# Attention scores on TensorE: a shared 128-row product over padded keys becomes twelve 64-row products

## The chip, the cores and the metric

The kernel runs on one core of a Trainium2 chip. The metric is the device time in microseconds (us) of one execution, the median of several. TensorE is called PE, its weight loads PEld, VectorE DVE, ScalarE ACT, GpSimd POOL, and SyncE, which issues the transfers, SP.

## The reference

An attention layer with a learned relative-position bias feeds a two-layer network. With 4 batches, 8 heads, 576 positions and a head dimension of 64:

```
scores = q @ k.T / 8                                   # 4 x 8 x 576 x 576
x      = log1p(|i - j|) / log1p(max(i, 1))
scores = scores + relu(x * w1 + b1) @ w2               # a bias for each head
attn   = softmax(scores)
h      = (attn @ v), heads side by side                # 2304 x 512
out    = relu(h @ w_in)**2 @ w_out                     # 512 -> 2048 -> 512
```

## The kernel before

Two batches are worked on together, as a pair `p`; batch `b` of the pair has its 64 head dimensions on partitions 64b to 64b+63, for queries and for keys. The 576 query rows of a batch are cut into chunks `c`: chunks 1 to 4 have 128 rows of each batch (the full blocks), chunk 0 has the last 64 rows of both batches together. A step `n` is one (pair, chunk, head); there are 2 x 5 x 8 = 80, and 64 of them are of full blocks. The order of all work is written out by hand in a string, `PROGRAM`, whose words name a piece of work and its argument ("qk:12", "kz:0.3"); every engine keeps that order.

Queries and keys are split into two 16-bit halves, so that a score is a sum of three products (`terms`: high x high, high x low, low x high). `qk(n)` makes the scores of a step in the PSUM tile `sc`, three banks of 512 columns, of which there is one. `softmax_a(n)` (L661) lets DVE add the bias, find the row minimum of the negated scores and write both batches' 576 columns to SBUF, one instruction for each batch; ACT then takes the exponential (L674). Later come the transposition (`turn` on PE for the first 16 steps, a transposing transfer after that), `pv` (L762, attention times values), and for each chunk the network: `g1` (L842), `square` (L854, L856, L862) and `g2` (L875).

For a full block, `qk` puts the scores of batch 0 at columns 0 to 575 of `sc` and those of batch 1 at columns 960 to 1535. So 512 columns of batch 0 fill bank 0, 512 of batch 1 fill bank 2, and the 64 columns left of each lie in bank 1. The part in bank 1 is made first, for both batches at once (L638): three products over all 128 partitions with 128 columns, whose moving operand `kz` holds batch 0's last 64 keys in its first 64 partitions and columns, batch 1's first 64 keys in the others, and zeros elsewhere. The other part follows as six products over 64 partitions each (L643), with 512 columns, alternating between the batches; `tile_position` puts the two batches on the upper and the lower half of the PE array.

`kz` is zeroed once by DVE (L903). `k_pad`, the word "kz" in `PROGRAM`, copies the keys of one head into it with two ACT instructions (L321), after `k_split` has made the halves on POOL or DVE; there are 16 heads in all (8 for each pair).

Of the kernel before, what the change touches and what calls it, by code (L numbers as in the profile page):

```python
# [9 lines left out]
F16 = mybir.dt.float16  # L10
# [19 lines left out]
ENG = {'kh': 'PPPPPPPAPPPPPPPP', 'kl': 'PPPPPPPPDDDDDDDD', 'vh': 'PPPPPPPAPPPPPPPP', 'vl': 'PPPPPPPPDDDDDDDD', 'wh': 'AAAAAAAA', 'wl': 'PPPPPPPP', 'wc': 'OOOOOOOO', 'wp': '01010101', 'qh': 'PPPPPPDDDDDDPPPPPPPP', 'ql': 'DDDDDDDDDDDDDDDDDDDD', 'ev': 'AAAAAAAAAAAAAAAAAAAAAAAAAAAADDDDDDDD', 'er': 'AAAAAAAAAAAAAAAAAAAAAAAAAAAADDDDDDDD', 'gh': 'PPPPPPPPPPPPPPPPDDDDDDDDDDDDDDDDDDDDDDDDDDDDDDDDDDDDDDDDDDDDDDDDDDDDDDDDDDDDDDDD', 'gl': 'PPPPPPPPPPPPPPPPPPPPPPPPPPPPPPPPPPPPPPPPPPPPPPPPPPPPPPPPPPPPPPPPPPPPPPPPPPPPPPPP', 'al': 'PPPPPPPPPPPPPPPPPPPPPPPPPPPPPPPPPPPPPPPPPPPPPPPPPPPPPPPPPPPPPPPPPPPPPPPPPPPPPPPP', 'oe': 'AAAAAAAAAAAAAAAAAAAA', 'kz': 'AAAAAAAAAAAAAAAA', 'te': 'AAAAAAAAAAAAAAAAAAAAAAAAAAAAAAAAAAAAAAAAAAAAAAAAAAAAAAAAAAAAAAAAAAAAAAAAAAAAAAAA', 'tt': 'AAAAAAAAAAAAAAAAAAAAAAAAAAAAAAAAAAAAAAAAAAAAAAAAAAAAAAAAAAAAAAAAAAAAAAAAAAAAAAAA', 'xe': 'AAAAAAAAAAAAAAAAAAAA', 'ah': 'AAAAAAAAAAAAAAAAAAAAAAAAAAAAAAAAAAAAHAAHAAHAAHAAHAAHAAHAAHAAHAAHAAHAAHAAHAAHAAHAAAA'}  # L30
# [6 lines left out]
NKZ = 8  # L37
# [6 lines left out]
BONE = False  # L44
PROGRAM = (
# [155 lines left out]
def tile_attention_moe(  # L201
# [99 lines left out]
    def k_split(p, h):  # L301
# [8 lines left out]
        else:  # L310
            nc.vector.scalar_tensor_tensor(
                out=t[:, 1, :], in0=st, scalar=float(2 ** KS), in1=t[:, 0, :],
                op0=ALU.mult, op1=ALU.subtract)

    def k_pad(p, h):
        t = k_t[p, h]
        for b in range(2):
# [687 lines left out]
```

## Time and profile before

| | |
|---|---|
| median of three runs | 639.39 us (638.95 to 641.38) |
| the profiled execution, its own time | 638.85 us |
| its span, first to last instruction | 637.2 us |
| mean granted clock of PE | 0.985 |
| busy: PE, PEld, DVE, ACT, POOL | 94%, 61%, 67%, 59%, 60% of the span |

The span begins with the first instruction and ends with the last; 1.65 us of the execution's time lie around it. A matmul's end is modelled from its size, and its duration covers the way through the array, so that matmuls that follow each other overlap in the listing; the distance from one start to the next is the better measure of what a matmul costs.

### The profile page before, as it was taken

The numbers are of one execution on the slowest core, as the hardware profiler recorded it, in microseconds if no ns is written. First come the engines' busy times: TensorE is split into PE (matmuls) and PEld (weight loads), VectorE is DVE, ScalarE is ACT, GpSimd is POOL, SyncE is SP. The second block draws the span as 40 slices with busy tenths as digits, with TensorE's granted clock in tenths as the row PEclk, the third lists the DMA queues.
The fourth block names the chain that finished last, engine by engine and source line by source line (L and its number), as shares of the span: only waits on it lengthen the run. The fifth ranks groups of instructions, "written<-read, shape, count | busy, mean of one in ns | idle before, by whom it ended". The sixth has DMA issues, their size and how long they took to land.

```text
span 637.2 us, 15498 instructions
## 1 busy us (share of the span) xinstructions
PE 601.6 (94%) x6056; PEld 385.7 (61%) x6056; DVE 426.4 (67%) x840; ACT 376.3 (59%) x811; POOL 384.8 (60%) x389
## 2 busy tenths in 40 slices
PE   5578998899999999999999999999999999999997
PEld 2135575664666477557556765766676676577564
DVE  7999999998679795787874663566456363613321
ACT  5679997769676365755567455746636575214020
POOL 5785599999766345766965646555665556523211
PEclk9779999999999999999999999999999999999999
DMA  8999987888799877798879768559975889512000
GB/s 289 342 309 294 284 257 229 259 192 186 167 193 199 181 167 181 162 235 200 191 159 231 149 130 185 133 115 192 183 142 121 150 172 163 121 39 71 17 34 17
DMA packets 204264, 112.16 MB, mean 176 GB/s; under 512 B 166816, under 2 KB 179104, under 8 KB 204192
## 3 DMA queue, kind: packets, MB, share of 16 engines
q1 hardware_dynamic: 204192, 111.18, 73.7%
q8 instruction: 47, 0.77, 0.5%
q14 instruction: 25, 0.20, 0.1%
HBM read 55.44 MB, written 15.61 MB: 111 GB/s over the span
## 4 chain that ended last, share of the span: by engine, by line
PE 67%; POOL 12%; DVE 7%; DMA 6%; issue 4%; ACT 3%; SPq 1%; POOLq 0%; DVEq 0%; ACTq 0%
PE o L875 25%; PE hp L842 25%; PE pv L762 7%; PE sc L643 5%; DMA kst<-kd 3%; POOL v L278 2%; DVE s L661 2%; PE bp L554 2%; DVE hg L489 2%; POOL cv L278 2%; POOL v L345 2%; PE sc L633 1%; POOL winL L406 1%; POOL g L862 1%; PE sc L638 1%
## 5 line engine op out<-in xcount | busy, mean ns | idle before, releaser
L842 PE MATMUL hp<-xt,winH 128*128 128x256 f16 (+1 forms) x1280 | 193.2, 262 | 1.4 <-DVE r L856 1.3
L875 PE MATMUL o<-woutH,g 128*128 128x512 f16 x576 | 184.8, 380 | 1.7 <-POOL g L862 1.0
L842 PE MATMUL hp<-xt,winL 128*128 128x256 f16 (+1 forms) x640 | 161.7, 262 | 0.0
L862 POOL TENSOR_TENSOR g<-r,g 128x512 f16<-128x512 f32 (+1 forms) x80 | 88.8, 1113 | 91.4 <-DVE g L280 78.6
L875 PEld LDWEIGHTS <-g 128*128 128x128 f16 x864 | 79.5, 98 | 98.9 <-issue 9.4
L842 PEld LDWEIGHTS <-winH 128*128 128x128 f16 x1280 | 117.9, 98 | 25.3 <-issue 8.5
L717 POOL TENSOR_TENSOR a<-s,a 128x1024 f16<-128x1024 f32 (+1 forms) x64 | 132.5, 2070 | 0.0
L661 DVE CUSTOM_DVE_ANT_0 s<-sc,bt 128x576 f32<-128x576 f32 x144 | 104.6, 749 | 35.3 <-PE sc L643 13.7
L856 DVE TENSOR_TENSOR r<-hp,r 128x512 f32<-128x512 f32 (+1 forms) x80 | 50.7, 634 | 108.4 <-ACT r L854 107.9
L875 PE MATMUL o<-woutL,g 128*128 128x512 f16 x288 | 109.2, 379 | 0.0
L674 ACT ACTIVATE s<-s,nm 128x576 f32<-128x576 f32 x120 | 92.9, 775 | 6.4 <-ACT nm L672 0.4
L854 ACT ACTIVATE r<-hp 128x512 f32<-128x512 f32 (+1 forms) x80 | 43.7, 546 | 85.9 <-PE hp L842 83.1
L715 POOL TENSOR_TENSOR a<-s,a 128x128 f16<-128x128 f32 (+1 forms) x64 | 29.8, 465 | 105.7 <-ACT a L276 76.2
L762 PE MATMUL pv<-v,at 128*128 128x64 f16 (+5 forms) x2112 | 88.0, 203 | 2.4 <-ACT at L276 1.3
L672 ACT ACTIVATE nm<-mx,esc 128x1 f32<-128x1 f32 x120 | 34.4, 287 | 77.9 <-DVE mx L661 77.5
L276 ACT ACTIVATE a<-s 128x1152 f16<-128x1152 f32 (+1 forms) x64 | 70.3, 1099 | 13.2 <-DMA at<-a 12.2
L842 PEld LDWEIGHTS <-winL 128*128 128x128 f16 x640 | 62.6, 98 | 5.8
L762 PEld LDWEIGHTS <-at 128*128 128x128 f16 (+1 forms) x1792 | 55.0, 100 | 16.8 <-issue 10.6
L489 DVE TENSOR_SCALAR hg<-tab_t 128x464 f32<-128x464 f32 (+17 forms) x88 | 60.0, 712 | 0.1
L280 DVE TENSOR_SCALAR g<-r 128x512 f16<-128x512 f32 (+1 forms) x64 | 46.6, 730 | 17.1 <-PE o L875 16.1
L643 PE MATMUL sc<-k,q 64*128 64x512 f16 x384 | 52.6, 379 | 0.0
L554 PE MATMUL bp<-hg,w2s 128*32 128x288 f32 (+15 forms) x152 | 36.3, 532 | 8.6 <-ACT hg L481 3.3
(90 smaller groups left out, 707.3 us busy)
## 6 DMA issues: line engine op xcount, KB each, us to landing
bt<-biasd SPq DMA_DIRECT2D x64, 288.0 KB, 3.6
stg<-w_in SPq DMA_DIRECT2D x16, 512.0 KB, 4.7
stg<-w_out SPq DMA_DIRECT2D x16, 512.0 KB, 5.6
biasd<-be SPq DMA_DIRECT2D x16, 295.5 KB, 5.3
bt<-biasd SPq DMA_DIRECT2D x32, 144.0 KB, 4.3
qst<-qd SPq DMA_DIRECT2D x32, 128.0 KB, 3.6
out<-o SPq DMA_DIRECT2D x16, 256.0 KB, 2.8
v<-vd SPq DMA_DIRECT2D x8, 320.0 KB, 7.0
```

Of the source, the lines that this page charges most:

```text
L276: nc.scalar.activation(out=out, in_=in_, func=AF.Copy, scale=scale)
L489: nc.vector.tensor_scalar(ht, src, scl[:, n:n + 1], None, op0=ALU.min)
L554: nc.tensor.matmul(out=bp[32 * t:32 * t + 32, 0:n], lhsT=w2s if gi < 4 or t < z else w2n, rhs=hg[gi, t][:, a0:a1, :] if gi in ONEP else hg ...
L643: nc.tensor.matmul(out=sc[:, 1024 * b:1024 * b + 512], lhsT=qt[r, qz, qs], rhs=kt[r, z, 64 * b:64 * b + 512], start=(m == 0), stop=(m == 2 ...
L661: nc.vector.tensor_tensor_reduce(s[:, 576 * b:576 * b + 576], sc[:, 960 * sb:960 * sb + 576], bt, inv, 3.0e38, ALU.add, ALU.min, mx[:, b:b ...
L674: nc.scalar.activation(out=sl, in_=sl, func=AF.Exp, scale=-1.0, bias=mx[:, b:b + 1] if f32 else nm[:, b:b + 1], accum_out=su[:, h, b:b + 1])
L717: eng.tensor_tensor(av[:, :, 640:1152], ev[:, :, 0:512], av[:, :, 0:512], op=ALU.subtract)
L762: nc.tensor.matmul(out=dst, lhsT=lhsT, rhs=rhs, start=b not in [x[1] for x in seq[:j]], stop=b not in [x[1] for x in seq[j + 1:]], tile_po ...
L842: nc.tensor.matmul(out=hp[:, f * T:f * T + T].rearrange("p (b t) -> p b t", b=nb), lhsT=wt[:, k, c0:c0 + 128], rhs=xt[:, 0:nb, z * 4 + k, ...
L856: nc.vector.tensor_tensor(rr, hp[:, 0:2 * T], rr, op=ALU.mult)
L862: eng.tensor_tensor(g[:, 1, 0:2 * T], rr, g[:, 0, 0:2 * T], op=ALU.subtract)
L875: nc.tensor.matmul(out=blk["o", b], lhsT=g[:, z, c0:c0 + 128], rhs=wt[:, 2 * u + f, :], start=(u == 0 and f == 0 and z == 0 and wt is wout ...
```

## The change

The padded copies are gone: the tile `kz`, its zeroing, `k_pad`, and the 32 words "kz" in `PROGRAM`. The other words keep their order.

The scores of batch 0 now lie at columns 64 to 639 of `sc`, those of batch 1 at 896 to 1471. Each batch has 448 columns in a bank of its own and 128 in bank 1. They are made with twelve products over 64 partitions each, in the order `SEQ`; an entry is (batch, own bank or not, term). While batch 0 makes its three products of 128 columns in bank 1, batch 1 begins with 448 columns in bank 2; at the end batch 1 makes its 128 columns in bank 1 while batch 0 finishes in bank 0. Both halves of the array write to bank 1, at different times: a `drain` behind batch 0's third product increments the semaphore `bank`, and PE waits for it ahead of batch 1's first product there. `fusable=True` allows the compiler to delete that drain and to put its increment on the instruction ahead of it.

```diff
+TM = 128
+SO = [512 - S + TM, 1024 - TM]
+SEQ = [(0, 0, 0), (1, 1, 0), (0, 0, 1), (0, 0, 2), (0, 1, 0), (1, 1, 1), (0, 1, 1), (1, 1, 2), (0, 1, 2),
+       (1, 0, 0), (1, 0, 1), (1, 0, 2)]
...
-    kz = const.tile([128, NKZ, 2, 128], F16, name="kz")
...
-    def k_pad(p, h):
-        t = k_t[p, h]
-        for b in range(2):
-            r = slice(64 * b, 64 * b + 64)
-            src = t[r, :, 512 - 512 * b:576 - 512 * b]
-            if zn("kz", p * 8 + h) == "A":
-                nc.scalar.activation(out=kz[r, h % NKZ, :, r], in_=src, func=AF.Copy)
-            else:
-                nc.vector.tensor_copy(kz[r, h % NKZ, :, r], src)
-            if b == 0:
-                yield
...
+    bank_sem, bank_n = ctx.enter_context(nc.semaphore("bank")), [0]
+    nc.tensor.sem_clear(bank_sem)
...
-            mid = sc[:, 512:1408].rearrange("p (b j) -> p b j", b=2)[:, :, 0:64]
-            for m, (qz, z) in enumerate(terms):
-                nc.tensor.matmul(out=mid, lhsT=qt[:, qz, qs], rhs=kz[:, h % NKZ, z, :],
-                                 start=(m == 0), stop=(m == 2))
-            for m, (qz, z) in enumerate(terms):
-                for b in range(2):
-                    r = slice(64 * b, 64 * b + 64)
-                    nc.tensor.matmul(out=sc[:, 1024 * b:1024 * b + 512], lhsT=qt[r, qz, qs],
-                                     rhs=kt[r, z, 64 * b:64 * b + 512],
+            for b, own, m in SEQ:
+                if (b, own, m) == (1, 0, 0):
+                    bank_n[0] += 1
+                    nc.tensor.wait_ge(bank_sem, bank_n[0])
+                r = slice(64 * b, 64 * b + 64)
+                if b:
+                    k0, w = (TM, S - TM) if own else (0, TM)
+                else:
+                    k0, w = (0, S - TM) if own else (S - TM, TM)
+                o = SO[b] + k0
+                qz, z = terms[m]
+                i = nc.tensor.matmul(out=sc[:, o:o + w], lhsT=qt[r, qz, qs], rhs=kt[r, z, k0:k0 + w],
                                      start=(m == 0), stop=(m == 2), tile_position=(64 * b, 0))
+                if (b, own, m) == (0, 0, 2):
+                    nc.tensor.drain(fusable=True).then_inc(bank_sem, 1)
...
-            sb = b if c else h % 2
+            sb = SO[b] if c else 960 * (h % 2)
             nc.vector.tensor_tensor_reduce(
                 s[:, 576 * b:576 * b + 576],
-                sc[:, 960 * sb:960 * sb + 576], bt, inv, 3.0e38, ALU.add, ALU.min, mx[:, b:b + 1])
+                sc[:, sb:sb + 576], bt, inv, 3.0e38, ALU.add, ALU.min, mx[:, b:b + 1])
...
-        nc.vector.memset(kz, 0.0)
-        yield
```

## Rows read from the trace of the kernel before

**Rows 1.** The page: busy time, share of the span, instructions.
```profile
PE 601.6 (94%) x6056; PEld 385.7 (61%) x6056; DVE 426.4 (67%) x840; ACT 376.3 (59%) x811; POOL 384.8 (60%) x389
```

**Rows 2.** Busy time of each engine in stretches of the span.
```profile
core 0: us, PE busy (x) PEld busy (x) DVE busy (x) ACT busy (x) POOL busy (x), PEclk, DMA share, GB/s
...
90.00:120.00 30.00, 26.49 (x240) 17.41 (x238) 28.24 (x57) 24.02 (x53) 28.37 (x37) 1.00 0.81 240
...
320.00:380.00 60.00, 59.98 (x666) 41.17 (x664) 36.06 (x77) 36.06 (x76) 33.74 (x28) 1.00 0.82 170
```

**Rows 3.** Waits of PE, 155 to 530 us: total us, times, longest.
```profile
PE hp L842 <- DVE r L856: 1.3, 1, 1.3
PE pv L762 <- DMA at<-a: 1.0, 1, 1.0
PE o L875 <- POOL g L862: 0.3, 1, 0.3
```

**Rows 4.** The chain that ended last: by engine, then pieces (start, us).
```profile
PE 67%; POOL 12%; DVE 7%; DMA 6%; issue 4%; ACT 3%; SPq 1%; POOLq 0%; DVEq 0%; ACTq 0%
...
63.90 0.75 PE sc L643 x6
...
70.04 0.75 PE sc L643 x6
...
165.10 0.27 PE sc L638 x3
165.37 0.75 PE sc L643 x6
166.13 0.92 PE pv L762 x28
...
518.45 0.75 PE sc L643 x6
```

**Rows 5.** Line 643 on PE in stretches: length, busy (count), clock.
```profile
60.00:155.00 95.00, 10.68 (x78) 1.00 0.82 239
155.00:320.00 165.00, 17.25 (x126) 1.00 0.85 186
320.00:520.00 200.00, 24.64 (x180) 1.00 0.78 159
```

**Rows 6.** PE's timeline round one step, from narrow windows: start, us.
```profile
309.86 0.38 PE L875 MATMUL o<-woutH,g 128*128 128x512 f16 x1
310.08 0.22 PE L638 MATMUL sc<-kz,q 128*128 128x128 f16 x1
...
310.13 0.28 PE L638 MATMUL sc<-kz,q 128*128 128x128 f16 x2
...
310.19 0.22 PE L638 MATMUL sc<-kz,q 128*128 128x128 f16 x1
310.34 0.82 PE L643 MATMUL sc<-k,q 64*128 64x512 f16 x6
...
310.78 0.38 PE L643 MATMUL sc<-k,q 64*128 64x512 f16 x2
311.09 0.39 PE L842 MATMUL hp<-xt,winH 128*128 128x256 f16 x2
```

**Rows 7.** Groups: line, engine, shape, count; busy us, mean ns; idle before.
```profile
L643 PE MATMUL sc<-k,q 64*128 64x512 f16 x384 | 52.6, 379 | 0.0
...
L638 PE MATMUL sc<-kz,q 128*128 128x128 f16 x192 | 21.2, 219 | 1.4 <-DVE mx L661 1.4
...
L321 ACT ACTIVATE kz<-k 64x128 f16<-64x128 f16 x32 | 9.8, 305 | 8.1 <-POOL k L309 4.4 <-DVE k L311 3.3
...
L903 DVE MEMSET kz<- 128x1024 uint32 x1 | 0.9, 912 | 0.2 <-issue 0.2
```

**Rows 8.** The chain's pieces up to 80 us: start, us.
```profile
46.69 0.20 ACT kz L321
46.90 0.31 ACT kz L321
...
49.49 0.20 ACT kz L321
49.70 0.31 ACT kz L321
...
75.95 0.63 POOL cv L278
```

**Rows 9.** The drains at the kernel's end on PE's queue: ns min/median/max, starts.
```profile
L1001 PEldq DRAIN  x2: 13/1496/2978, 629.6 to 636.7; - x2
```

**Rows 10.** PE's timeline, its last matmuls.
```profile
631.95 0.38 PE L875 MATMUL o<-woutL,g 128*128 128x512 f16 x1
632.16 0.38 PE L875 MATMUL o<-woutH,g 128*128 128x512 f16 x1
```

More of the change, by code (lines that the diff above doesn't have):

```diff
@@ L27 @@
 LB = 1152
-ENG = {'kh': 'PPPPPPPAPPPPPPPP', 'kl': 'PPPPPPPPDDDDDDDD', 'vh': 'PPPPPPPAPPPPPPPP', 'vl': 'PPPPPPPPDDDDDDDD', 'wh': 'AAAAAAAA', 'wl': 'PPPPPPPP', 'wc': 'OOOOOOOO', 'wp': '01010101', 'qh': 'PPPPPPDDDDDDPPPPPPPP', 'ql': 'DDDDDDDDDDDDDDDDDDDD', 'ev': 'AAAAAAAAAAAAAAAAAAAAAAAAAAAADDDDDDDD', 'er': 'AAAAAAAAAAAAAAAAAAAAAAAAAAAADDDDDDDD', 'gh': 'PPPPPPPPPPPPPPPPDDDDDDDDDDDDDDDDDDDDDDDDDDDDDDDDDDDDDDDDDDDDDDDDDDDDDDDDDDDDDDDD', 'gl': 'PPPPPPPPPPPPPPPPPPPPPPPPPPPPPPPPPPPPPPPPPPPPPPPPPPPPPPPPPPPPPPPPPPPPPPPPPPPPPPPP', 'al': 'PPPPPPPPPPPPPPPPPPPPPPPPPPPPPPPPPPPPPPPPPPPPPPPPPPPPPPPPPPPPPPPPPPPPPPPPPPPPPPPP', 'oe': 'AAAAAAAAAAAAAAAAAAAA', 'kz': 'AAAAAAAAAAAAAAAA', 'te': 'AAAAAAAAAAAAAAAAAAAAAAAAAAAAAAAAAAAAAAAAAAAAAAAAAAAAAAAAAAAAAAAAAAAAAAAAAAAAAAAA', 'tt': 'AAAAAAAAAAAAAAAAAAAAAAAAAAAAAAAAAAAAAAAAAAAAAAAAAAAAAAAAAAAAAAAAAAAAAAAAAAAAAAAA', 'xe': 'AAAAAAAAAAAAAAAAAAAA', 'ah': 'AAAAAAAAAAAAAAAAAAAAAAAAAAAAAAAAAAAAHAAHAAHAAHAAHAAHAAHAAHAAHAAHAAHAAHAAHAAHAAHAAAA'}
+ENG = {'kh': 'PPPPPPPAPPPPPPPP', 'kl': 'PPPPPPPPDDDDDDDD', 'vh': 'PPPPPPPAPPPPPPPP', 'vl': 'PPPPPPPPDDDDDDDD', 'wh': 'AAAAAAAA', 'wl': 'PPPPPPPP', 'wc': 'OOOOOOOO', 'wp': '01010101', 'qh': 'PPPPPPDDDDDDPPPPPPPP', 'ql': 'DDDDDDDDDDDDDDDDDDDD', 'ev': 'AAAAAAAAAAAAAAAAAAAAAAAAAAAADDDDDDDD', 'er': 'AAAAAAAAAAAAAAAAAAAAAAAAAAAADDDDDDDD', 'gh': 'PPPPPPPPPPPPPPPPDDDDDDDDDDDDDDDDDDDDDDDDDDDDDDDDDDDDDDDDDDDDDDDDDDDDDDDDDDDDDDDD', 'gl': 'PPPPPPPPPPPPPPPPPPPPPPPPPPPPPPPPPPPPPPPPPPPPPPPPPPPPPPPPPPPPPPPPPPPPPPPPPPPPPPPP', 'al': 'PPPPPPPPPPPPPPPPPPPPPPPPPPPPPPPPPPPPPPPPPPPPPPPPPPPPPPPPPPPPPPPPPPPPPPPPPPPPPPPP', 'oe': 'AAAAAAAAAAAAAAAAAAAA', 'te': 'AAAAAAAAAAAAAAAAAAAAAAAAAAAAAAAAAAAAAAAAAAAAAAAAAAAAAAAAAAAAAAAAAAAAAAAAAAAAAAAA', 'tt': 'AAAAAAAAAAAAAAAAAAAAAAAAAAAAAAAAAAAAAAAAAAAAAAAAAAAAAAAAAAAAAAAAAAAAAAAAAAAAAAAA', 'xe': 'AAAAAAAAAAAAAAAAAAAA', 'ah': 'AAAAAAAAAAAAAAAAAAAAAAAAAAAAAAAAAAAAHAAHAAHAAHAAHAAHAAHAAHAAHAAHAAHAAHAAHAAHAAHAAAA'}
 PATS = ["DDDD", "ADDD", "AADD", "DDDP", "DDPP", "ADDP", "ADPP", "AADP", "AAPP", "DPPP"]
@@ L36 @@
 ORDER = [[0, 3, 2, 4, 1], [1, 4, 2, 3, 0]]
-NKZ = 8
 NF = 16
@@ L942, in tile_attention_moe @@
     work = {"st": start, "tb": tables, "sc": scales, "hc": hconst, "rs": rowscale, "hg": hgen, "bm": bias_mm,
-            "bo": bias_out, "bl": bias_ld, "qd": q_dma, "qs": q_split, "kd": k_dma, "ks": k_split, "kz": k_pad,
+            "bo": bias_out, "bl": bias_ld, "qd": q_dma, "qs": q_split, "kd": k_dma, "ks": k_split,
             "vd": v_dma, "vs": v_split, "wd": w_dma, "ws": w_split, "qk": qk, "sa": softmax_a, "sb": softmax_b,
```

295 rows, old and new, of the table PROGRAM are left out of this document.

## The prediction

> **What bounds the kernel now.** I read the page's busy times first, then the stretches, PE's waits, the chain, and last the start times of single matmuls inside one step. The page says that PE is busy for 94% of the span and that no other engine passes 67% [rows 1]. An average over stages is not yet a bound, so the stretches come next: from 90 to 120 us POOL and DVE each work 28 of 30 us while PE has more air; from 320 to 380 us PE is busy 59.98 of 60 us, while DVE and ACT work 36.06 each and POOL less [rows 2]. The boundary is near 155 us. From there to 530 us PE waits 2.6 us in all for other engines, in three places [rows 3]. So in the second stage a microsecond of PE work is nearly a microsecond of time, and in the first it is not.
>
> The chain says the same and counts for me. 67% of it is PE. Between 160 and 530 us it runs through the scores of 43 steps; the first piece, with the mid products before it, and the last are shown, and in the first stage two more steps are on it [rows 4]. Line 643 has six matmuls a step, so the 126 and 180 of the stretches are 51 steps in the second stage, and the 78 ahead of it are 13 [rows 5]. Eight of the 51 therefore lie beside a stretch in which something else came last.
>
> **What one step costs now.** The timeline gives it to two decimals [rows 6]. The three mid products start at 310.08, 310.13 and 310.19, so 128 columns cost 0.055 us. The first 64-row product starts 0.15 after the last mid product, 0.095 more than its columns need: going from 128 rows to 64 costs that much. The pairs start at 310.34 and the third pair at 310.78, so a pair, two products of 512 columns on the two halves, costs 0.22 (line 875's 512 columns cost 0.215, [rows 10]); the halves really run side by side. From the last pair to the next line's first matmul are 0.31, which is 0.095 over the pair's columns: the way back to 128 rows. The sum is 0.11 + 0.15 + 0.44 + 0.31 = 1.01; the chain's pieces give 0.27 + 0.75 = 1.02 [rows 4]. I take 1.02. The step into the mid products is free: 310.08 less 309.86 is just the 512 columns before.
>
> **What one step will cost.** All twelve products are 64-row ones. The price of going to 64 rows is still paid once, now at the front: 0.095. The columns scale: 448 cost 0.215 x 448/512 = 0.188, 128 cost 0.055. Batch 0's half has 3 x 0.055 + 3 x 0.188 = 0.73; batch 1's half has the same work in another order. If the two halves run freely beside each other the step's columns take 0.73 instead of 0.11 + 0.055 + 0.65, and the way back is 0.095 again. Sum: 0.095 + 0.73 + 0.095 = 0.92, so 0.10 less by these rounded figures, and I use 0.095. There are three more weight loads a step; in `pv` 28 load-and-multiply pairs take 0.92, so a pair can follow another in 0.033, below the 0.055 of the shortest product here [rows 4]. I cost the loads at nothing; if 64-row loads could not run ahead, three times 0.033 would eat the gain.
>
> **The semaphore.** If the compiler puts the increment on batch 0's third product, no instruction is left that holds PE. That product starts about 0.11 into the columns; as modelled it ends 0.22 later [rows 7], at 0.33. Batch 1's first product in bank 1 is due when its two further products of 448 columns are through, at 3 x 0.188 = 0.56. The wait is over 0.2 us ahead of its turn: nothing. Queued behind it on PE are only this step's last two products and then the next line, and DVE's two reductions, which wait for them. The rows show no wait of this kind inside a step, so its price lies between nothing and the drain's, below; I take nothing, since the order leaves 0.23.
>
> **DVE and the rest.** The reductions read 576 columns as before, released by the end of the step as before. PE's first product of the next step writes to bank 1, which both reductions read, as did the mid products; no wait is added there.
>
> **ACT's copies.** 32 instructions of 305 ns go, 9.8 us, and ACT stood 8.1 us before them, because it waits in order for the key halves [rows 7]. In the second stage PE's work covers both. In the first, four of the copies stand on the chain: 0.20 + 0.31 twice, 1.02 us [rows 8]. They lead to POOL's stretch from 75.95 on, which can start so much earlier if nothing else comes last: between 0 and 1.0 us, and I take 1.0. Of the waits more could come back, up to 4.4 us for those on POOL, if the order behind them tightened; that is the bound below. DVE's zeroing, 0.9 us, happens while the first transfers are under way; I cost it at nothing.
>
> **Sum.** 43 steps on the chain in the second stage x 0.095 = 4.1 us, with all 51 it would be 4.8. Two steps in the first: 0.2. The copies: 1.0. Together 5.3 us. The profiled execution took 638.85 us, span and surroundings together; 638.85 - 5.3 = 633.6. The median of the runs is 0.54 above it, so 634.1; I write **634.2 us**, 0.8% below. The likeliest case's own range is 632.5 to 636.2, the upper end for a sum in which a third is absorbed.
>
> **Rivals.**
>
> *The halves do not run freely (slower).* Rows 6 show only pairs of equal length. If products had to finish in the order they were issued, the short products of one half could not overtake a long one of the other. Then batch 0's second product ends no earlier than batch 1's first of 448 columns, at 0.19; the third ends at 0.245; two rounds of 0.188 bring 0.62; batch 0's last product of 448 columns ends at 0.81, the first product of 128 with it, and two more of 0.055 come to 0.92. The step is then 0.095 + 0.92 + 0.095 = 1.11, 0.09 more than now: 43 to 51 steps give 3.9 to 4.6 us, less 1.0 for the copies, about +3.3: 642.7 us. It decides as soon as the two halves lose more than 0.1 us to each other in a step. For it: no unequal pair in the trace. Against it: the two products of a pair share their time without loss, 0.22 for both where one alone costs 0.215, so each half has a path of its own for its columns, and a matmul's listed end is modelled, not seen.
> [...]
>
> *The drain stays (slower).* The drain at the kernel's end shows what one does on PE: it was taken up at 629.6 and lasted 2.978 us, to 632.58 [rows 9], while the last matmul began at 632.16 and ended, as modelled, at 632.54 [rows 10]. So it holds the queue until PE is through, 0.42 after the last start, some 0.2 after the last columns. Inside a step it would wait for batch 1's 448 columns (0.19) plus 0.2, and I add 0.05 (an estimate, half of the 0.095 of a change of rows) for the restart: 0.44, then 3 x 0.188 = 0.56, with both changes of rows 1.19. That is 0.17 more than now; 43 to 51 steps give 7.3 to 8.7 us, less 1.0: 646 to 647 us. Against it: the drain is marked so that its increment may move to a product that carries no other. For it: nothing in the trace.
>
> *The gain is absorbed.* PE runs earlier and meets transfers and POOL, which have 6% and 12% of the chain [rows 4]. 2.6 us of waiting [rows 3] would have to grow by more than 2. Then 636.5 to 639.
>
> **Chances.** Free halves and a moved increment: 0.63. Absorbed: 0.14. In order of issue: 0.13. The drain stays: 0.10. A change under 0.5% (3.2 us: below 636.2 or above 642.6 counts) is about what this measurement cannot tell from none. Of the first case I give 0.60 to faster and 0.03 to same; of the absorbed 0.02 and 0.12; of the ordered 0.04 to same and 0.09 to slower; the drain is slower. That makes 0.62, 0.19 and 0.19. The range takes the first two cases and most of the third: 632.0 to 643.5 us, which leaves out the drain and the tails.
>
> **What would show it.** In the trace after, a step of 0.92 from the first score product to the next line's start, with short products of one half starting 0.055 apart while the other half streams: right. Short products that start only when the other half's 448 columns are through, and a step of 1.11: the first rival. A drain on PE's queue in every step and a gap of about 0.2 after the fourth product: the second. Steps of 0.92, but PE's waits after 155 us grown by microseconds: the third. The first stage is judged by when the long run of POOL on the chain begins: 75.95 now, about 75 after. A time over 637 would mean that one of these steps failed; one under 632, that ACT's waits ahead of the copies had held up far more than the chain shows.

## The result

| | before | changed |
|---|---|---|
| median | 641.13 us (638.95 to 644.94, 8 runs) | 635.21 us (633.33 to 637.72, 8 runs) |
| ratio, 95% interval | | 0.9897 [0.9868, 0.9927] |
| the profiled execution, its span | 638.85, 637.2 us | 635.0, 633.2 us |
| 51 steps of the second stage: first score product to the line after the last | 354.11 us | 348.30 us |

The medians here are of runs side by side. The forecast of 634.2 us took 5.3 us off the profiled execution of 638.85 and added 0.54 for the median of the runs then known, 639.39; the median beside the changed kernel is 641.13. Between the medians of this table the change saves 5.9, and by the interval of the ratio 4.7 to 8.5 (641.13 x 0.0073 and x 0.0132). The profiled execution of before lies at the fast end of its kernel's runs.

The page of the changed kernel, busy times and the chain by engine, which answer to [rows 1] and [rows 4]:

```profile
PE 595.9 (94%) x6248; PEld 397.4 (63%) x6248; DVE 426.1 (67%) x839; ACT 367.0 (58%) x779; POOL 384.2 (61%) x389
...
PE 61%; DVE 13%; DMA 11%; POOL 5%; ACT 4%; issue 4%; SPq 1%; DVEq 0%; ACTq 0%; POOLq 0%
```

PE is still the engine that is full. It has 192 matmuls and 192 weight loads more (64 steps, twelve products in place of nine), and is busy 5.7 us less. ACT has lost its 32 copies. POOL has 5% of the chain where it had 12, DVE 13 where it had 7, and DMA 11 where it had 6, though POOL's and DVE's busy times are what they were (384.2 and 426.1 us, before 384.8 and 426.4); such shares alone say little.

PE's waits between 155 and 530 us, which answer to [rows 3]:

```profile
PE hp L836 <- DMA xt<-xh: 0.8, 1, 0.8
PE hp L836 <- DVE r L850: 0.5, 1, 0.5
PE bp L541 <- DVE hg L476: 0.3, 1, 0.3
PE o L869 <- POOL g L856: 0.2, 1, 0.2
```

They come to 1.8 us where they were 2.6. What PE saved was not taken back as waiting.

One step of the changed kernel, which answers to [rows 6]. First the timeline of PE round it (the group of twelve carries the name of its first shape), then line 636 in its first 0.16 us, with the shapes at the end:

```profile
306.79 0.38 PE L869 MATMUL o<-woutH,g 128*128 128x512 f16 x1
307.10 0.91 PE L636 MATMUL sc<-k,q 64*128 64x128 f16 x12
307.94 0.28 PE L836 MATMUL hp<-xt,winH 128*128 128x256 f16 x1
```

```profile
L636 PE MATMUL sc<-k,q x4: 216/221/360, 307.1 to 307.2; 64*128 64x128 f16 x3, 64*128 64x448 f16 x1
```

Then line 636 in narrow stretches, where (x) counts the products that are listed as running; a count that rises by one between two stretches is a product that has started:

```profile
core 0: us, PE busy (x), PEclk, DMA share, GB/s
307.09:307.15 0.06, 0.05 (x2) 1.00 2.83 303
307.17:307.21 0.04, 0.04 (x3) 1.00 0.21 39
307.23:307.27 0.04, 0.04 (x4) 1.00 0.00 0
307.28:307.30 0.02, 0.02 (x5) 1.00 1.39 115
307.31:307.32 0.01, 0.01 (x6) 1.00 0.00 0
```

Two products start together at 307.10: a short one of batch 0 and a long one of batch 1. The second and third short products start at about 307.16 and 307.22, while that long one is still streaming: the next product of batch 1 starts only at 307.30. In this step the short products of batch 0 don't wait for batch 1's long one. From the starts as the trace lists them, to the ns, a step is: 0.097 more than before behind the matmul ahead of it (0.312 from its start in place of 0.215), twelve products that start 0, 0.003, 0.066, 0.122, 0.178, 0.203, 0.367, 0.392, 0.556, 0.581, 0.637 and 0.693 after the first, and 0.148 from the last start to the next line, of which 0.056 are its columns. That is 0.842 inside and 0.938 with the entry; before it was 1.017. The starts are the medians of the 51 steps of the stage. Three of the 51 follow a bias product (line 541); the distance from it to the step is what it was before (0.48 to 0.53), so that they pay no entry more. The steps save 51 x (1.017 - 0.842) - 48 x 0.097 = 4.3 us.

The drains on PE's queue are still only those of the kernel's end:

```profile
L993 PEldq DRAIN  x2: 13/1490/2968, 625.7 to 632.8; - x2
```

In the trace batch 0's third product carries the increment, and the wait sits on the weight load of batch 1's first short product. That load starts at 307.535, 0.437 into the step (the trace shows its start, not the moment of the increment), between these two stretches of line 636 on PEld:

```profile
core 0: us, PEld busy (x), PEclk, DMA share, GB/s
307.50:307.53 0.03, 0.03 (x1) 1.00 1.29 230
307.54:307.58 0.04, 0.04 (x2) 1.00 1.16 173
```

### The profile page after: what moved, and what is told of

Read it like the earlier page. It is cut to its first block, busy times and chain, and to the rows that moved or that the text cites. A ratio compares the mean times of both kernels' runs of the same rounds, so it can differ in the third digit from the quotient of the medians.

```text
span 633.2 us, 15857 instructions
## 1 busy us (share of the span) xinstructions
PE 595.9 (94%) x6248; PEld 397.4 (63%) x6248; DVE 426.1 (67%) x839; ACT 367.0 (58%) x779; POOL 384.2 (61%) x389
## 4 chain that ended last, share of the span: by engine, by line
PE 61%; DVE 13%; DMA 11%; POOL 5%; ACT 4%; issue 4%; SPq 1%; DVEq 0%; ACTq 0%; POOLq 0%
PE hp L836 23%; PE o L869 23%; PE pv L756 6%; PE sc L636 6%; DMA xt<-xh 3%; PE bp L541 2%; DVE s L655 2%; DMA at<-a 2%; DMA bt<-biasd 2%; DMA qst<-qd 2%; DVE hg L476 2%; ACT s L668 1%; POOL g L856 1%; DVE ci L363 1%; DMA stg<-w_out 1%
## 5 line engine op out<-in xcount | busy, mean ns | idle before, releaser
L636 PE MATMUL sc<-k,q 64*128 64x128 f16 (+1 forms) x768 | 58.2, 284 | 1.3 <-DVE mx L655 1.3
L636 PEld LDWEIGHTS <-q 64*128 64x128 f16 x768 | 39.6, 94 | 28.1 <-issue 19.0
```

What stands on the lines that cost most here:

```text
L636: i = nc.tensor.matmul(out=sc[:, o:o + w], lhsT=qt[r, qz, qs], rhs=kt[r, z, k0:k0 + w], start=(m == 0), stop=(m == 2), tile_position=(64 * ...
```

## The experiments

Times are medians; "stage" is the second stage of the profiled execution, as in the first table (354.11 before), "step" one full-block step with its entry.

| run | median us | before beside it | ratio, 95% interval | step | stage |
|---|---|---|---|---|---|
| e1_changed_again | 634.04 | 641.13 | 0.990 [0.987, 0.993] | 0.938 | 348.95 |
| e8_changed_third | 634.51 | 640.92 | 0.991 [0.988, 0.994] | 0.938 | 349.72 |
| e2_copies_back | 636.16 | 641.13 | 0.992 [0.989, 0.995] | 0.938 | 349.15 |
| e9_copies_back_again | 636.27 | 640.92 | 0.992 [0.988, 0.995] | 0.938 | 351.24 |
| e5_before_no_copies | 642.13 | 640.60 | 1.001 [0.997, 1.005] | 1.017 | 354.07 |
| e3_drain_stays | 648.47 | 641.13 | 1.012 [1.008, 1.016] | 1.225 | 362.23 |
| e4_wait_early | 644.51 | 641.13 | 1.006 [1.003, 1.009] | 1.186 | 358.85 |
| e6_halves_in_turn | 636.74 | 640.60 | 0.993 [0.990, 0.997] | 0.949 | 349.88 |
| e10_one_half_after_the_other | 640.71 | 641.78 | 0.998 [0.995, 1.001] | 1.065 | 353.97 |
| e7_64_and_512 | 633.63 | 640.60 | 0.989 [0.984, 0.995] | 0.938 | 348.53 |

### The change once more, twice

> The changed kernel as it is, beside the kernel before on the same chip, as the measure for the other runs. Ratio to before 0.99, as first measured; a step of the scores from its first product to the next line 0.84 us, and PE's path through the second stage (from the first of its steps to the last) some 4 to 5.6 us shorter. Nothing is told apart by it alone.

> The changed kernel once more, as the partner of the copies put back on the same chip and in the same rounds: 634 to 636 us, ratio to before about 0.99.

The kernel is the changed one, unaltered. The ratios, 0.990, 0.990 and 0.991, agree. What the profiles show beside it is how loose the first stage is: the first step of the second stage began at 165.03 us before, and at 166.28, 168.92 and 166.38 in three profiles of the same changed kernel. Over all kernels of the table it lies between 164.3 and 169.3. A term of one microsecond in the first stage can't be read from a single profile.

### The copies

Back into the changed kernel went the tile `kz`, its zeroing, `k_pad` and the 32 words; nothing reads them.

```diff
+    kz = const.tile([128, NKZ, 2, 128], F16, name="kz")
...
+    "... bm:3.1 vd:0.5 rs kz:0.0 rs hg:0.0 kd:0.2 kz:0.0 hg:1.1 ..."
```

> The changed kernel with the tile of padded keys, its zeroing and ACT's 32 copies put back at their old places; no product reads them. Theory A (the gain is PE's: 51 steps, each shorter by 0.08 us, and the copies are hidden, since the changed kernel's POOL reaches the same places between 75 and 125 us as before): the time of the changed kernel within 0.2%, ratio to before about 0.99. My prediction's sum: 1.0 us slower than the changed kernel (0.16%). Theory B (the copies, and what waits behind them on ACT, make up the 2.6 us by which the measured gain exceeds 51 x 0.08): 2.6 us slower (0.4%), ratio 0.994.

> The changed kernel with ACT's copies put back, again, because the first comparison (636.16 against 634.04, spreads of 5 us) did not tell 0 from 2.6 us. Theory A (hidden): the two runs together differ by less than 0.8 us. The prediction's sum: 1.0. Theory B: 2.6 us slower again.

The other way round, the kernel before lost its 32 words "kz" and kept all else, so that its products read zeros where the copies should stand:

> The kernel before with ACT's 32 copies left out and all else as it was: its products over the padded keys read zeros, so the scores of 64 keys of each batch lack their product. It is the other side of the copies put back. Theory A (hidden): within 0.15% of the kernel before. My prediction's sum: 1.0 us faster, ratio 0.9984. Theory B (the copies carry what the measured gain has over 51 x 0.08): 2.6 us faster, ratio 0.996.

Put back, the copies cost 2.1 and 1.8 us in the medians (634.04 to 636.16, 634.51 to 636.27) and 1.2 and 1.1 in the means, but by the ratios only 0.2% and 0.03%, with intervals that overlap nearly whole. Taken from the kernel before, they gave nothing: 1.001 [0.997, 1.005], an interval that leaves out theory B's 0.996 but not the 0.998 of the prediction's sum. So they are worth between nothing and about 2 us; the runs don't settle where.

ACT's timeline shows where the expected microsecond goes. Before, at the place of [rows 8], one pair of copies stands ahead of the weights' copy (`woutH`), the other between it and the exponential:

```profile
45.62 1.07 ACT L580 ACTIVATE be<-bp,hcst,rows_s 128x351 f32<-128x351 f32 x2
46.59 0.62 ACT L321 ACTIVATE kz<-k 64x128 f16<-64x128 f16 x2
47.23 0.63 ACT L276 ACTIVATE woutH<-cv 128x512 f16<-128x512 f32 x1
...
49.39 0.62 ACT L321 ACTIVATE kz<-k 64x128 f16<-64x128 f16 x2
50.03 0.60 ACT L276 ACTIVATE at<-tp 128x512 f32<-128x512 f32 x1
50.65 0.62 ACT L485 ACTIVATE hg<-tab_t 128x384 f32<-128x384 f32 x1
51.17 0.76 ACT L674 ACTIVATE s<-s,mx 128x576 f32<-128x576 f32 x1
```

The changed kernel, same place; the brackets are ACT's idle time and who ended it:

```profile
46.18 1.07 ACT L567 ACTIVATE be<-bp,hcst,rows_s 128x351 f32<-128x351 f32 x2
47.14 0.62 ACT L275 ACTIVATE woutH<-cv 128x512 f16<-128x512 f32 x1
47.66 0.60 ACT L472 ACTIVATE hg<-tab_t 128x368 f32<-128x368 f32 x1
48.16 0.58 ACT L275 ACTIVATE at<-tp 128x512 f32<-128x512 f32 x1
48.63 0.60 ACT L472 ACTIVATE hg<-tab_t 128x368 f32<-128x368 f32 x1
49.13 0.74 ACT L275 ACTIVATE at<-tp 64x128 f32<-64x128 f32 x2
50.13 0.62 ACT L472 ACTIVATE hg<-tab_t 128x384 f32<-128x384 f32 x1 [0.26 <-PE bp L541]
51.20 0.78 ACT L668 ACTIVATE s<-s,mx 128x576 f32<-128x576 f32 x1 [0.45 <-DVE mx L655]
```

The last piece starts at 51.20 in place of 51.17. Two pairs of copies are gone, 1.24 us; 0.7 of it comes back as ACT's waits for PE and DVE, and the rest this execution had already lost ahead of the place (the weights' copy at 47.14 would have come 0.62 earlier than 47.23 by the missing pair alone, and came 0.09 earlier). Counted from the start of the pair `be` to that of the exponential, which leaves out what was lost ahead, the stretch takes 5.55 us before and in both runs with the copies put back, and 5.02, 4.87, 4.47 and 5.05 in the four profiles without them (the change three times, and the kernel before without its copies). So 0.5 to 1.1 of the 1.24 us are gained on the spot; the traces don't show how much of that reaches the end of the kernel.

### The drain stays

```diff
-                    nc.tensor.drain(fusable=True).then_inc(bank_sem, 1)
+                    nc.tensor.drain(fusable=False).then_inc(bank_sem, 1)
```

> The changed kernel with fusable=False, so that a drain stands in every step behind batch 0's third product. By the prediction's price, PE stands until batch 1's 448 columns are through (0.19) and 0.2 more, and 0.05 to start again, so the step grows by 0.25 to 0.27 us: 51 steps give 13 to 14 us, ratio to before 1.010 to 1.013. If a drain only held PE's queue and the array had work left, nothing or under 2 us would be seen. The profile should list 64 more drains on PE's queue.

This is the prediction's second rival, built. The drain's line in the trace, and line 636 round a step that begins at 313.11:

```profile
L639 PEldq DRAIN  x64: 398/1738/3498, 64.8 to 526.1; - x64
```

```profile
313.11:313.15 0.04, 0.04 (x2) 1.00 0.18 58
313.24:313.30 0.06, 0.06 (x4) 1.00 0.72 192
313.31:313.34 0.03, 0.03 (x4) 1.00 0.00 0
313.50:313.56 0.06, 0.00 (x0) 1.00 0.96 307
313.56:313.58 0.02, 0.01 (x2) 1.00 0.87 346
```

Now there are 64 drains. Four products start and nothing else until PE is empty (x0); the next two start 0.460 and 0.466 into the step. Batch 1's first 448 columns are through at 0.003 + 0.189 = 0.19, so 0.27 pass in this step from the last column, by this estimate, to the next start. The step is 1.225, the kernel 1.2% slower than before. The prediction had 0.44, 1.19 and 646 to 647 us for this case, 6.3 to 7.7 above before; 648.5 were measured, 7.3 above.

### The wait early

```diff
-SEQ = [(0, 0, 0), (1, 1, 0), (0, 0, 1), (0, 0, 2), (0, 1, 0), (1, 1, 1), (0, 1, 1), (1, 1, 2), (0, 1, 2),
-       (1, 0, 0), (1, 0, 1), (1, 0, 2)]
+SEQ = [(0, 0, 0), (1, 1, 0), (0, 0, 1), (0, 0, 2), (0, 1, 0), (1, 0, 0), (1, 0, 1), (1, 0, 2), (0, 1, 1), (1, 1, 1), (0, 1, 2), (1, 1, 2)]
```

> The changed kernel with another order of the twelve products: batch 1's three products in bank 1, behind the wait, come right after batch 0's first of 448 columns; then two pairs of 448 follow. It tells whether the wait is free only where it stands. Theory A: the wait lasts until batch 0's third product has ended (0.12 + 0.22 = 0.34 into the step, plus the way of the semaphore), so batch 1's product, which could start at 0.20, starts at about 0.40 to 0.45, everything behind it moves, and the step grows by about 0.2 us: 51 steps give 10 us, ratio to before about 1.005. Rival: the wait costs nothing anywhere (a half is never held by the other's completion), and only the poorer packing is paid: batch 0's second product of 448 columns is queued behind the three short ones and starts at 0.37 or a little later; under 0.05 us a step, under 3 us, ratio 0.995 or less.

Batch 1's short products, and with them the wait, come right behind batch 0's first long one, so that the increment is late by design and shows in the starts. Line 635 (the order has one line less) in a step that begins at 308.88:

```profile
309.01:309.05 0.04, 0.04 (x4) 1.00 0.77 173
309.07:309.30 0.23, 0.23 (x5) 1.00 0.51 190
309.33:309.35 0.02, 0.02 (x3) 1.00 1.48 346
```

Five products have started by 309.07, and none does until 309.32: batch 1's first short one starts at 0.440, batch 0's next long one at 0.450. The product with the increment started at 0.122, so the product behind the wait starts 0.32 after it, 0.26 after its 128 columns (0.056). Batch 0's next long one, which by its columns could have started at 0.178 + 0.19 = 0.367, as it does in the changed kernel, starts 0.08 later; three products of batch 1 were issued ahead of it, no more than were passed in the two orders below. Whether the wait itself holds it, the starts don't show. In the changed kernel the same product is due at 0.581, and its weight load, which carries the wait, starts at 0.437: the slack is 0.14, and the wait costs nothing, as predicted.

### The halves in turn, and one after the other

If each half only kept pace with the other because `SEQ` alternates, other orders should cost time. First batch 0's three short products and its first long one ahead of batch 1's first, then all six of batch 0 ahead of all six of batch 1:

```diff
+SEQ = [(0, 0, 0), (0, 0, 1), (0, 0, 2), (0, 1, 0), (1, 1, 0), (0, 1, 1), (1, 1, 1), (0, 1, 2), (1, 1, 2), (1, 0, 0), (1, 0, 1), (1, 0, 2)]
```

```diff
+SEQ = [(0, 0, 0), (0, 0, 1), (0, 0, 2), (0, 1, 0), (0, 1, 1), (0, 1, 2), (1, 1, 0), (1, 1, 1), (1, 1, 2),
        (1, 0, 0), (1, 0, 1), (1, 0, 2)]
```

> The changed kernel with its twelve products in the plain order: batch 0's three in bank 1 alone, then three pairs of 448 columns, then batch 1's three in bank 1 alone. It takes away only the unequal overlap. Theory A (the step's gain comes from short products of one half running under a long one of the other): the columns take 0.01 + 3 x 0.056 + 3 x 0.189 + 3 x 0.056 = 0.91 instead of 0.75, the step with both changes of rows 1.10, 0.08 more than before: 51 steps give 4 us, ratio to before 1.004 to 1.007, about 8 us above the changed kernel. Rival (the overlap is worth little, the change gains by what it takes from ACT and from the mid products): within 2 us of the changed kernel, ratio 0.993 or less.

> Only the order of the twelve products is changed again: all six of batch 0 (three of 128 columns, three of 448) are issued ahead of all six of batch 1 (three of 448, three of 128). In the run with the halves in turn, a product issued fifth started 0.013 us into the step, ahead of two issued before it. Theory A, a half's products pass those of the other half without limit: batch 1's first product, issued seventh, starts within 0.03 us of batch 0's first, the step stays at 0.85 inside (0.95 with the change of rows at its start), and the time lies within 2 us of the changed kernel (634 to 637). Theory B, PE looks only a few products ahead: batch 1's first starts after one to three of batch 0's, at 0.06 to 0.37, and ends as much later; the step grows by 0.05 to 0.3, and with 51 steps on the path the time is 637 to 650. Theory C, the overlap seen so far came from something else and the order of issue holds: batch 1 starts only at 0.65 to 0.73, the step is about 1.45, and 51 steps cost about 26 us: some 660.

The expectation for the halves in turn fell: the step is 0.949 and the kernel as fast as the changed one, within the intervals. Its line 635, first 0.06 us and then first 0.17 us of a step that begins at 311.60:

```profile
L635 PE MATMUL sc<-k,q x2: 226/292/359, 311.6 to 311.6; 64*128 64x128 f16 x1, 64*128 64x448 f16 x1
...
L635 PE MATMUL sc<-k,q x4: 216/221/359, 311.6 to 311.7; 64*128 64x128 f16 x3, 64*128 64x448 f16 x1
```

The four products issued first are 128, 128, 128 and 448 columns of batch 0. What starts is one short product, then at 0.013 one of 448 columns, then the two other short ones at 0.066 and 0.122. The long one can't be batch 0's own: that half goes on at its usual pace (0.066, 0.122, then 448 columns at 0.177, 0.367, 0.556), and a second series follows the early one (0.013, 0.213, 0.402). It is batch 1's, issued fifth, and it started ahead of three that were issued before it (the expectation of the other run, above, says two).

With all of batch 0 ahead, line 636 in the first 0.06 and the first 0.15 us of a step that begins at 345.55, and in narrow stretches:

```profile
L636 PE MATMUL sc<-k,q x1: 226/226/226, 345.6 to 345.6; 64*128 64x128 f16 x1
...
L636 PE MATMUL sc<-k,q x4: 216/221/361, 345.6 to 345.7; 64*128 64x128 f16 x3, 64*128 64x448 f16 x1
```

```profile
345.56:345.61 0.05, 0.05 (x1) 1.00 1.09 410
345.62:345.67 0.05, 0.05 (x2) 1.00 1.38 532
...
345.69:345.72 0.03, 0.03 (x4) 1.00 0.88 341
```

Batch 1's first product, issued seventh, starts at 0.130, right behind the start of batch 0's third at 0.122. Again exactly three that were issued ahead of it had not started. Everything of batch 1 comes 0.13 later, the step ends at 0.13 + 0.84 = 0.97 and costs 1.065 with its entry, 0.05 more than before; the time is that of before, 0.998 [0.995, 1.001], as PE waits less outside the steps (below). The start at 0.130 lies in the range of theory B of the expectation (0.06 to 0.37). In both orders the first product of batch 1 started with three of batch 0, issued ahead of it, not yet started; why it is three, and whether it is so in other orders, no run shows.

### 64 and 512 columns

```diff
-TM = 128
+TM = 64
```

> The changed kernel with 64 and 512 columns in place of 128 and 448. The columns of a half stay 1728 in sum. If only their sum counts, the step stays at 0.84 and the time at that of the changed kernel (ratio 0.99). If a product of 64 columns is bound by its weight load instead (0.033 as in pv, in place of 0.027), six of them in a half's path cost at most 0.02 a step more, 1 us. If the loads of one half can not run ahead under the other's products, the short products start further apart than 0.05 us and the step grows by 0.1 and more.

The same columns for each half, cut 3 x 64 and 3 x 512. The short products start 0.029 apart, the step is 0.938 again, and the time equals that of the changed kernel within the interval. It is the lowest median of all, by 0.4 us, which these runs can't tell from nothing. No kernel tried beats the change.

## Why the prediction was right

**The bound.** PE after 155 us: right. The stage shrank by 5.8 us in the profile after, by 5.2 and 4.4 in the two repeats; PE's waits in it did not grow in sum (2.6 before, 1.8 after, 2.1 and 2.4 in the repeats).

**The step.** Predicted 0.92 from 0.095 + 0.73 + 0.095; measured 0.097 + 0.749 + 0.092 = 0.938. The two changes of rows were sized right from the trace of before. The columns take 0.02 more, half of it because the first product of a half takes 0.01 more than the next ones: batch 0's first short one 0.066 in place of 0.056, batch 1's first long one 0.200 in place of 0.189 (its long ones start at 0.003, 0.203 and 0.392), where the sum had 0.055 and 0.188 for each. The saving is 0.079 a step where 0.095 was used. Both kernels pay both changes of rows, so what went is padding: a half streams 3 x (128 + 448) = 1728 columns in place of 3 x (128 + 512) = 1920, and 192 columns, at 0.189 for 448, are 0.081. The prediction took 43 steps for the sum and 51 as its upper end: all 51 count, and 48 of them pay the entry. 43 x 0.095 = 4.1 and the 4.3 counted here agree because a saving that was too large met a count that was too small.

**The semaphore.** No cost: right, but by a thinner margin. The prediction let the increment come at the product's modelled end, 0.33, with a slack of 0.23; the load that waits for it starts at 0.437, with a slack of 0.14. The wait moved earlier shows what lies beyond that: 1.186 - 1.017 = 0.17 a step more than before.

**The weight loads.** 192 more of them cost nothing that shows: PEld is busy 11.7 us more, and the products of a half still start one behind the other, 0.056 apart for 128 columns.

**The copies.** This term is not shown. One microsecond was put down for ACT's copies, because the chain ran through them. The sign named for it did not come: POOL's piece at 75.95 stands at 75.99 in the profile after. But it stands at 77.07 in another profile of the same kernel, so a microsecond can't be read from it either way. The chain goes through ACT there, but PE or DVE then end part of the same stretch, and on the spot 0.5 to 1.1 us are gained, as the timelines above show. For the whole kernel the runs hold anything from nothing to 2 us, the 1.0 included.

**The sum.** 5.3 us were forecast, 5.9 measured between the medians, 6.5 as the mean of three pairs (5.9, 7.1, 6.4). The steps give 4.3, and the second stage 4.4 to 5.8 in the three profiles. The difference is waiting that went: outside the 51 steps and the distances into them, the same matmuls of the stage take PE 294.2 us from start to start before, and 292.6, 293.1 and 293.9 in the three profiles of the changed kernel. Why PE waits less there no run shows. Behind the stage 0.5 is lost again (118.6 us in place of 118.1 to the end of the span). What is left, 1 to 2 us, would lie in the first stage, where the copies and the 0.2 of its two steps were; it varies by 5 us between profiles, so this stays open. That the saving came out within 1.2 us of the forecast is in part luck: a count too small, a saving too large and a term for the copies that no run pins down.

**The rivals.** *Halves in order of issue*: wrong. The step is 0.938 and not 1.11, and in the timeline after the short products start at 0.066 and 0.122 inside the other half's long one. There the twelve start in the order of issue; in the two changed orders products overtook others at their start too: with the halves in turn a product issued fifth started 0.013 us into the step, ahead of three issued before it. *The drain stays*: it didn't; where it was made to, its price was as worked out (0.46 for 0.44). *The gain absorbed*: no; PE's waits fell. In the slower variants, too, PE waits less than before: 51 steps of the drain cost 51 x 0.111 + 48 x 0.097 = 10.3 us, and the stage grew by 8.1; those of the early wait 8.3, and it grew by 4.7; those of one half after the other 2.2, and it did not grow. What is missing lies outside the steps, where the stage takes 292.0, 290.7 and 292.0 us in these three in place of 294.2.

## What to carry to other kernels

Here the products over 64 rows on the two halves of the array could be costed for each half by itself, in columns (0.749 us in the changed kernel), plus 0.097 + 0.092 = 0.19 for going from 128 rows to 64 and back. The order of issue counted where all six of one half stood ahead of all six of the other: a step of 1.065 in place of 0.938. Twelve products without padding took 0.079 us a step less here than nine with it. Where the two halves must be ordered by a semaphore, note that 0.32 us passed here between the start of the product that signals and that of the one that waits, put as much of other products between them, and look in the trace whether a drain that may be removed was removed. A copy on the chain need not be worth its length: on the spot 0.5 to 1.1 of 1.24 us were gained here, so look at the times of the engines that are nearly late before counting the whole copy.

## What the runs showed of the hardware that was not expected

- PE started a product of one half ahead of three products of the other half that were issued before it, and in neither order of more: with the halves in turn, issued fifth, it started at 0.013 us with three still waiting; with one half after the other, issued seventh, at 0.130, when three were left.
- With the wait early, the first product behind it started 0.32 us after the start of the product that carries the increment, 0.26 after its 128 columns and 0.1 after its modelled end. In the changed kernel the waiting weight load started 0.315 after that start (0.437 less 0.122). With the wait early, the other half's next long product started at 0.450, in the changed kernel at 0.367.
- With a drain between products, 0.27 us passed on PE from the last column (0.19, worked out) to the next start (0.460).
- With 64 and 512 columns, products of 64 columns over 64 rows start 0.029 us apart; those of 128 columns start 0.056 apart in the changed kernel: half the columns, half the distance.
